# The second half of expert 1 for sequences 0 and 1, moved from the early stage into two more periods of the paired scheme

## The chip, the core and the metric

The kernel runs on one core of a Trainium2 chip. The metric is the time on the device in microseconds (us); of the kernel before, three runs are given, and one further execution was profiled. PE is the matrix engine (TensorE), DVE the VectorE, ACT the ScalarE, POOL the GpSimd; SP issues DMA transfers.

## What is computed

A gated linear attention, and then a mixture of experts with a balanced routing matrix. All numbers are float32 at the interface; the kernel splits each into two float16 parts ("high" and "low") and forms three products of four.

```python
# attention: batch 4, 8 heads, 768 tokens, head size 48
f = 1/(1 + exp(-f_logit))
state = f[:, :, t, :, None]*state + einsum('bhd,bhe->bhde', k[:, :, t], v[:, :, t])
y[:, :, t] = einsum('bhd,bhde->bhe', q[:, :, t], state)
# x: the 3072 tokens by 384 columns of all heads
P = exp(x @ w_gate - max)                  # 8 experts
for _ in range(8):                         # rows and columns brought to their sums in turn
    P /= P.sum(1, keepdims=True) + 1e-9;  P /= P.sum(0, keepdims=True) + 1e-9;  P *= N/E
for e in range(8):
    out += P[:, e:e+1] * (maximum(x @ w1[e], 0) @ w2[e])   # w1: 384x1024, w2: 1024x384
```

## The kernel before

**Three stages.** The attention stage goes through 24 items (a sequence has six, of 128 tokens each; a unit `u` is half a sequence, three items). It is paced by steps `g` of 0 to 208: every step advances each live item by one `yield`, and then calls `fill(n)`, which issues `n` units of plain expert work on PE, so that PE has work while the other engines carry out the attention. Items 3 to 23 start eight steps apart; item `i` runs its first ACT operation (`ft`) at step 23 + 8(i-3) and its score products (`aps`) twelve steps later. The second stage is the balancing of the routing matrix (`balance`, 38 steps: six, then four for each of eight iterations). Each iteration ends in a matmul `sk_c` that adds over the partitions what DVE has reduced into `sk_cs`; DVE takes up `sk_c` before the next iteration. Each of these steps also calls `fill` with 6.9 units, and goes on after the 38 for as long as there are units. The third stage is one loop of periods, listed in `ORDER`.

**The plain way and the paired way.** The plain way is matmul upon matmul: `moe` treats a unit of 384 tokens, with 9 matmuls of 384 columns for each of the hidden blocks `f` and 3 for each block and tile on the way back; `moe_tile` treats 128 tokens, and is used for units 0 to 2 (`TILED = 3`), because their tokens come late: a group of four hidden blocks is 36 matmuls of 128 columns, and the way back 3 matmuls of 384 columns for each block. A unit of `fill` is one matmul of 384 columns or three of 128. For each group, ACT writes the high part (`hh`) and DVE the low part (`hl`). The paired way does one half (`m`) of an expert for one sequence (`b`) in one period with fewer products: 15 slots of 6 matmuls of 256 columns (`kb_A` to `kb_F`), and three blocks of 42 matmuls of 192 columns (`kyps`, `kxps`), 216 matmuls in all; sums and differences of weights and tokens (`k1s`, `xs`) are made beforehand on POOL, and split into `k1h`, `k1l`, `xah`, `xal`.

**What goes which way.** Experts 0 and 1 go the plain way (they fill the attention stage), experts 2 to 7 the paired way: 6 x 2 x 4 = 48 periods. Of expert 1 the second half of the hidden blocks (`m = 1`) of sequences 2 and 3 also goes the paired way (`HALVED`), in periods 49 and 50. `plain(e, u)` tells `moe` how many of the eight hidden blocks are left for it.

**What sets the order.** The code's own order: `pin` and `mm` chain the instructions of an engine in the order in which they are written, so an engine that waits holds up all that is written behind it. `FILL` gives the units of each step from a step on, and the plain work may not run ahead of its tokens ("an expert is ahead of its tokens"). `load` brings one quarter of a weight matrix, has ACT make the high part and DVE the low (`w1l`, `w2l`, line 385); `SECONDAT` gives the steps of these two for the eight quarters of expert 1. In the balancing stage, when the first 14 pairs of `RAW` are done, the pool `kw` opens, and in the next step `prepare_w1` begins on two quarters of expert 2: sums on POOL, a maximum (`wmx`) and four low parts (`k1l`) on DVE.

Of the kernel before, what the change touches and what calls it, by code (L numbers as in the profile page):

```python
# [26 lines left out]
FT = FF // 128  # L27
# [51 lines left out]
END = 27  # L79
W1AT = (0, 1, 2, 3, 5, 9, 10, 11, 12, 21, 23, 25, 26)  # L80
W1AT0 = (16, 18, 19, 19, 22, 23, 23, 27, 27, 33, 35, 40, 41)
W2AT = (4, 22, 25, 25, 27, 29, 30, 35, 38)
W2AT0 = (0, 1, 1, 3, 3, 5, 5, 5, 7)
W2AT1 = (3, 8, 10, 12, 13, 13, 14, 14, 19)
# [7 lines left out]
CONVAT = (3, 6, 7, 9, 11)  # L92
LAST_EVENTS = {18: (('gs', 'C', 1, 1), ('gs', 'C', 1, 2), ('hl', 'C', 1)), 19: (('gs', 'C', 1, 3), ('gf', 'F', 2), ('gh', 1, 0), ('gh', 1, 1))}
ENDING = '.0.1.01.1..12.1.22..23.23.34343444'
HALVED = (2, 3)
ORDER = [(e, m, b) for e in range(2, NE) for m in range(2) for b in range(B)] + [(1, 1, b) for b in HALVED]
PAIRED = (0, 1, 2)
BY_POOL = (1,)
# [9 lines left out]
TS = CT * C  # L108
ONES = CT * NP * D * 4
LEADS = 23  # L110
FILL = ((0, 11.7), (1, 10.3), (2, 0), (3, 0), (5, 2), (6, 0), (7, 6), (8, 6), (9, 0), (10, 6), (12, 5.3), (15, 5.3), (17, 5.3), (23, 8.7), (30, 8.7), (43, 8.0), (195, 7))
LEAD = 6.9
FIRSTAT = ((0,), (0,), (0, 4), (0, 7), (1, 9), (5, 10))
SECONDAT = ((16, 17), (18, 20), (17, 18), (17, 21), (20, 21), (20, 22), (24, 24), (24, 25))
# [169 lines left out]
def fast(ctx, tc, qkf, vbd, wg, w1, w2, out, flag):  # L284
# [10 lines left out]
    def behind(ins, first):  # L295
        tc.add_manual_dep(
            ins.ins, first.ins.name,
            mybir.DependencyInfo(mybir.DependencyClass.NoSync, mybir.DependencyReason.DATA),
            reason="issue order")
# [3 lines left out]
    def pin(ins):  # L303
        engine = ins.ins.engine
        if fixed[0]:
            if engine in last:
                behind(ins, last[engine])
            last[engine] = ins
        return ins

    def mm(transpose=False, **kw):
        ins = (nc.tensor.transpose if transpose else nc.tensor.matmul)(**kw)  # L312
        if order:
            behind(ins, order[-1])
        order.append(ins)
# [6 lines left out]
    wctx, wctx0, wctx2, actx, pctx = (ExitStack() for _ in range(5))  # L322
    wp2 = wctx2.enter_context(tc.tile_pool(name="wp2", bufs=4, side="right"))
    wp1 = wctx.enter_context(tc.tile_pool(name="wp1", bufs=4, side="right"))
    wp0 = wctx0.enter_context(tc.tile_pool(name="wp0", bufs=8, side="right"))
    ap = actx.enter_context(tc.tile_pool(name="ap", bufs=2, side="right"))
    dp = ctx.enter_context(tc.tile_pool(name="dp", bufs=1, space=DRAM))
    psm = ctx.enter_context(tc.tile_pool(name="psm", bufs=2, space=PSUM))
# [7 lines left out]
    for h in range(2):  # L336
        nc.gpsimd.affine_select(
            out=mask[h * 64:(h + 1) * 64], in_=mask[h * 64:(h + 1) * 64],
# [27 lines left out]
    def xof(u):  # L366
        return [x[:, :, u % 2, :] for x in xt[u // 2]]

    def load(e, k, j):
        src = (w1 if k == 1 else w2)[e, j]  # L370
        n = 4 * (k - 1) + j
        if n < 6:
            raw = xp.tile([128, 1152], F32, name=f"w{k}r_{e}_{j}", tag=f"x{'hl'[n % 2]}{3 - n // 2}", bufs=1)[:, 0:768]
        else:
            raw = rp.tile([128, 768], F32, name=f"w{k}r_{e}_{j}", tag="wraw", bufs=3)
        raw = raw.rearrange("p (a f) -> p a f", f=256 if k == 1 else DM)
        nc.sync.dma_start(out=raw, in_=src)
        yield
        wh, wl = ((wp0 if e else wp1 if k == 1 else wp2).tile(list(raw.shape), F16, name=f"w{k}{q}_{e}_{j}", tag=f"w{q}") for q in "hl")
        scale = W1S if k == 1 else W2S  # L380
        pin(nc.scalar.activation(out=wh, in_=raw, func=AF.Copy, scale=scale))
        pair = [wh, None]
        ws[e][k - 1][j] = pair
        yield
        pin(nc.vector.scalar_tensor_tensor(out=wl, in0=raw, scalar=scale, in1=wh, op0=ALU.mult, op1=ALU.subtract))  # L385
        pair[1] = wl
# [10 lines left out]
    def plain(e, u):  # L397
        return FT // 2 if e == 1 and u // 2 in HALVED else FT

# [42 lines left out]
    tiles, put_off, owed = [0], [False], []  # L442

    def moe_tile(e, u, t):
        w1s, w2s = ws[e]
        if (u, t) not in ready:
            raise RuntimeError("an expert is ahead of its tokens")
        xh, xl = xof(u)
        ts = slice(t * 128, t * 128 + 128)
        h = []  # L450
        for g in range(2):
            ps = bank([128, 4, 128], f"hps_{e}_{u}_{t}_{g}")
            n = 0
            for q, x in ((0, xh), (0, xl), (1, xh)):
                for f in range(4 * g, 4 * g + 4):
                    a = w1s[f // 2][q]
                    fs = slice((f % 2) * 128, (f % 2) * 128 + 128)
                    for k in range(KT):
                        mm(out=ps[:, f % 4, :], lhsT=a[:, k, fs], rhs=x[:, k, ts], start=(n == 0), stop=(q == 1 and k == KT - 1), skip_group_check=True)
                        n += 1  # L460
                        if n < 36:
                            yield 1 / 3
            i = tiles[0] % FT
            tiles[0] += 1
            th, tl = (hp.tile([128, 2, 256], F16, name=f"h{q}_{e}_{u}_{t}_{g}", tag=f"k{q}{i // 6}{i % 6 // 3}{i % 3}").rearrange("p c t -> p (c t)") for q in "hl")
            pf = ps.rearrange("p f t -> p (f t)")
            pin(nc.scalar.activation(out=th, in_=pf, func=AF.Relu))

            def low(tl=tl, pf=pf, th=th):
                pin(nc.vector.scalar_tensor_tensor(out=tl, in0=pf, scalar=0.0, in1=th, op0=ALU.max, op1=ALU.subtract))  # L470

            if put_off[0]:
                owed.append(low)
            else:
                low()
            h.append([v.rearrange("p (f t) -> p f t", t=128) for v in (th, tl)])
            yield 1 / 3
        ps = bank([128, DM], f"yps_{e}_{u}_{t}")
        n = 0
        for f in range(FT):  # L480
            if len(owed) > 1 - f // 4:
                raise RuntimeError("a low part is owed")
            wh, wl = w2s[f // 2]
            hh, hl = (v[:, f % 4, :] for v in h[f // 4])
            for a, b in ((hh, wh), (hh, wl), (hl, wh)):
                mm(out=ps, lhsT=a, rhs=b[:, f % 2, :], start=(n == 0), stop=(n == 3 * FT - 1))
                n += 1
                if n < 3 * FT:
                    yield 1
        yr = rp.tile([128, DM], F32, name=f"yr_{e}_{u}_{t}", tag="yraw", bufs=3)  # L490
        pin(nc.scalar.activation(out=yr, in_=ps, func=AF.Copy))
        nc.sync.dma_start(out=yscr[e][u, t * 128:(t + 1) * 128], in_=yr)
        yield 1
# [596 lines left out]
        return (lambda: xq), lambda: sums(b), [x32[:, k].rearrange("p u t -> p (u t)") for k in range(KT)]  # L1090

    first = [load(0, 1 + n // 4, n % 4) for n in range(8)]
    second = [load(1, 1 + n // 4, n % 4) for n in range(8)]
    wgen = gate_weights()
    it = early_item(0)
    go(it)
# [22 lines left out]
    live, g = [it, nxt], 0  # L1119
    for n in range(2, 8):  # L1120
        at_steps(first[n], *FIRSTAT[n - 2])
    for n in range(8):
        at_steps(second[n], 4 + n, *SECONDAT[n])
    begin = {LEADS + STEPS * (i - 3): i for i in range(3, NT)}
    begin_tail = max(begin) + 17
    while live or g < max(begin):
# [14 lines left out]
        put_off[0] = g < PUTOFF  # L1141
        fill([n for at_, n in FILL if g >= at_][-1])
        go_all(g)
# [325 lines left out]
    for n, (e, m, b) in enumerate(ORDER):  # L1469
        part = n % 4  # L1470
        if n - part + 4 < PERIODS and part in (0, 2):
            e2, m2, _ = ORDER[n - part + 4]
            gen = prepare_w1(e2, 2 * m2 + part // 2)
            at_all(n, W1AT if n else W1AT0, gen)
        if n == 0:
# [214 lines left out]
```

## Time and profile before

| | |
|---|---|
| median of 3 runs | 1459.27 us (1458.95 to 1459.32) |
| the profiled execution: its own time | 1458.97 us |
| its span, first to last instruction | 1457.2 us |
| busy: PE, DVE, ACT, POOL | 1435.4, 1241.6, 1112.2, 1092.3 us |
| granted TensorE clock, mean | 0.997 |

The own time is 1.8 us more than the span, and 0.3 us below the median of the runs. An engine's busy time counts stretches in which at least one of its instructions runs; matmuls overlap each other, so that the time of one in a row is longer than the distance from one to the next.

### The profile page before, as it was taken

Reading aid. Unit: us, or ns where it says so; the run is one execution under the profiler, and the core shown is the slowest. Engines: PE = TensorE matmul, PEld = TensorE weight load, DVE = VectorE, ACT = ScalarE, POOL = GpSimd, SP = SyncE. Lnnn points to the kernel's source line nnn. Section 1 sums busy time; section 2 is a strip of 40 time slices with the busy share of each in tenths; the row PEclk is TensorE's granted clock in tenths of the full one; section 3 lists DMA queues with packets and bytes.
Section 4 is the critical chain, followed back from the end, with each engine's and each line's share of the span. In section 5 each row is a group of like instructions: output and inputs, shape, how many; then the busy total and the mean of one; then the engine's idle time right before and its main releaser. Section 6 shows DMA issues by size and latency. Waiting matters only on the chain.

```text
span 1457.2 us, 40795 instructions
## 1 busy us (share of the span) xinstructions
PE 1435.4 (99%) x16188; PEld 1267.0 (87%) x16188; DVE 1241.6 (85%) x2540; ACT 1112.2 (76%) x2492; POOL 1092.3 (75%) x1288
## 2 busy tenths in 40 slices
PE   7999999999999999999999999999999999999997
PEld 5788886666568899999999999999999999999997
DVE  8868878877868998888899898888888889888886
ACT  7767778875547778888888888888777787778874
POOL 3244665675625769999999999999888888888874
PEclk9999999999999999999999999999999999999999
DMA  9245544541111011222211111111000000000201
GB/s 265 84 113 132 120 110 126 124 120 47 65 49 35 24 40 47 56 62 61 61 55 58 49 50 45 41 51 49 23 23 24 23 23 23 13 15 20 77 13 69
DMA packets 82955, 90.54 MB, mean 62 GB/s; under 512 B 50017, under 2 KB 69601, under 8 KB 82754
## 3 DMA queue, kind: packets, MB, share of 16 engines
q1 hardware_dynamic: 82322, 87.25, 21.6%
q8 instruction: 128, 2.10, 0.6%
q14 instruction: 73, 0.60, 0.1%
q10 hardware_dynamic: 432, 0.59, 0.1%
HBM read 64.03 MB, written 14.16 MB: 54 GB/s over the span
## 4 chain that ended last, share of the span: by engine, by line
PE 73%; DVE 3%; ACT 1%; POOL 0%; issue 0%; ACTq 0%; POOLq 0%; DVEq 0%
PE kyps L312 29%; PE kb_A L312 9%; PE kb_B L312 8%; PE kb_D L312 6%; PE kxps L312 5%; PE kb_C L312 4%; PE yps L312 4%; PE hps L312 3%; PE kb_E L312 2%; PE kb_F L312 2%; DVE k1l L1228 0%; DVE kf L1538 0%; DVE kl L1569 0%; POOL k1s L1216 0%; DVE acc L1387 0%
## 5 line engine op out<-in xcount | busy, mean ns | idle before, releaser
L312 PEld LDWEIGHTS <-k1h 128*128 128x128 f16 x3000 | 282.5, 98 | 21.4 <-issue 1.1
L312 PE MATMUL kyps<-k2h,kgl 128*128 128x192 f16 x1188 | 292.3, 246 | 0.6 <-POOL kgl L1564 0.6
L312 PE MATMUL kyps<-k2h,kgh 128*128 128x192 f16 x1188 | 292.3, 246 | 0.1
L312 PE MATMUL kyps<-k2l,kgh 128*128 128x192 f16 x1188 | 292.2, 246 | 0.0
L312 PEld LDWEIGHTS <-kgh 128*128 128x128 f16 x2400 | 220.9, 98 | 7.2 <-issue 0.5
L1564 POOL TENSOR_TENSOR kgl<-kf,kgh 128x512 f16<-128x512 f32 x148 | 198.4, 1341 | 2.1 <-ACT kgh L1561 2.1
L1387 DVE SCALAR_TENSOR_TENSOR yy<-kyps,pes,part 128x192 f32<-128x192 f32 x270 | 111.5, 413 | 92.5 <-PE kyps L312 82.3
L1564 POOL TENSOR_TENSOR kgl<-kr,kgh 128x512 f16<-128x512 f32 x148 | 175.4, 1185 | 9.1 <-PE kyps L312 7.7
L1430 POOL TENSOR_TENSOR acc<-acc,yy 128x384 f32<-128x384 f32 x135 | 134.9, 1000 | 58.4 <-DVE yy L1387 58.4
L312 PEld LDWEIGHTS <-k1l 128*128 128x128 f16 x1500 | 146.8, 98 | 16.9
L312 PEld LDWEIGHTS <-kh 128*128 128x128 f16 x1200 | 112.6, 98 | 7.9 <-issue 1.3
L312 PEld LDWEIGHTS <-kgl 128*128 128x128 f16 x1200 | 117.4, 98 | 0.9 <-POOL kgl L1564 0.8
L312 PEld LDWEIGHTS <-w1h 128*128 128x128 f16 x1248 | 87.9, 98 | 27.1 <-issue 2.1
L312 PE MATMUL yps<-w2h,hl 128*128 128x384 f16 x336 | 110.1, 328 | 1.0 <-DVE hl L470 0.9
L312 PE MATMUL yps<-w2l,hh 128*128 128x384 f16 x336 | 110.0, 328 | 0.6 <-DVE w2l L385 0.6
L312 PE MATMUL yps<-w2h,hh 128*128 128x384 f16 x336 | 110.1, 328 | 0.2 <-ACT hh L420 0.2
L1515 ACT ACTIVATE cp<-kb_A 128x512 f32<-128x512 f32 x150 | 89.8, 599 | 17.5 <-DVE kb_A L1517 15.9
L1541 POOL TENSOR_TENSOR kr<-kr 128x256 f32<-128x256 f32 x100 | 75.6, 756 | 33.5 <-DVE xbl L1029 26.4
L312 PEld LDWEIGHTS <-hh 128*128 128x128 f16 x672 | 65.1, 99 | 37.2 <-issue 1.0
L1384 ACT ACTIVATE kyps<-kyps 128x192 f32<-128x192 f32 x148 | 47.7, 322 | 65.2 <-PE kyps L312 65.1
L1561 ACT ACTIVATE kgh<-kf 128x512 f16<-128x512 f32 x150 | 94.9, 633 | 1.7 <-DVE kf L1538 1.6
L1561 ACT ACTIVATE kgh<-kr 128x512 f16<-128x512 f32 x150 | 94.3, 629 | 0.6 <-DVE kr L1538 0.6
(323 smaller groups left out, 5383.6 us busy)
## 6 DMA issues: line engine op xcount, KB each, us to landing
q<-in_qkf_dram SPq DMA_DIRECT2D x23, 672.0 KB, 5.0
k1r<-in_w_dram SPq DMA_DIRECT2D x26, 384.0 KB, 3.0
k2r<-in_w_dram SPq DMA_DIRECT2D x26, 384.0 KB, 3.0
ys<-yr SPq DMA_DIRECT2D x48, 192.0 KB, 2.4
yb<-ys SPq DMA_DIRECT2D x48, 192.0 KB, 2.4
vr<-in_vbd_dram SPq DMA_DIRECT2D x24, 192.0 KB, 2.5
out_dram<-acc SPq DMA_DIRECT2D x21, 192.0 KB, 1.9
w1r<-in_w_dram SPq DMA_DIRECT2D x8, 384.0 KB, 9.4
```

What stands on the lines that cost most here:

```text
L312: ins = (nc.tensor.transpose if transpose else nc.tensor.matmul)(**kw)
L1384: pin(nc.scalar.activation(out=out, in_=in_, func=AF.Copy, **kw))
L1387: pin(nc.vector.scalar_tensor_tensor(out=y, in0=ps, scalar=p, in1=z, op0=ALU.mult, op1=ALU.add))
L1430: pin(nc.gpsimd.tensor_tensor(out=y, in0=y, in1=z.rearrange("p s d -> p (s d)"), op=ALU.add))
L1515: pin(nc.scalar.activation(out=fresh(ev[2]), in_=bk, func=AF.Copy))
L1541: pin((nc.gpsimd if ev[2] == 'P' else nc.vector).tensor_tensor(out=r[:, 0], in0=r[:, 1], in1=r[:, 0], op=ALU.subtract))
L1561: pin(nc.scalar.activation(out=hs['g', t][0][i], in_=hs['f' if i else 'r', t], func=AF.Copy))
L1564: pin((nc.vector if tag == str(PERIODS - 1) and ev[1] else nc.gpsimd).tensor_tensor(out=hs['g', t][1][i], in0=hs['f' if i else 'r', t], in ...
```

## The change

`HALVED` names all four sequences, so that `ORDER` has 52 entries. Of expert 1 the plain way then keeps only hidden blocks 0 to 3 everywhere; `moe_tile` learns of it by `plain`. The last two quarters of both weight matrices of expert 1 are no longer loaded and split ahead of the attention (`second` has four entries in place of eight), and the pool `wp0` is half as large. `FILL` hands out fewer units per step, and the slots `W1AT0` of the first period's weight work are spread anew.

```diff
-W1AT0 = (16, 18, 19, 19, 22, 23, 23, 27, 27, 33, 35, 40, 41)
+W1AT0 = (16, 18, 19, 19, 22, 23, 23, 25, 26, 26, 29, 37, 40)
-HALVED = (2, 3)
+HALVED = (0, 1, 2, 3)
 ORDER = [(e, m, b) for e in range(2, NE) for m in range(2) for b in range(B)] + [(1, 1, b) for b in HALVED]
-FILL = (..., (12, 5.3), (15, 5.3), (17, 5.3), (23, 8.7), (30, 8.7), (43, 8.0), (195, 7))
+FILL = (..., (12, 5.3), (15, 5.3), (17, 5.3), (23, 5.2), (43, 6.7), (107, 7.5), (195, 6.5))
-    wp0 = wctx0.enter_context(tc.tile_pool(name="wp0", bufs=8, side="right"))
+    wp0 = wctx0.enter_context(tc.tile_pool(name="wp0", bufs=4, side="right"))
     # moe_tile
-        for g in range(2):
+        fts = plain(e, u)
+        for g in range(fts // 4):
...
-        for f in range(FT):
-            if len(owed) > 1 - f // 4:
+        for f in range(fts):
+            if len(owed) > fts // 4 - 1 - f // 4:
...
-                mm(out=ps, lhsT=a, rhs=b[:, f % 2, :], start=(n == 0), stop=(n == 3 * FT - 1))
+                mm(out=ps, lhsT=a, rhs=b[:, f % 2, :], start=(n == 0), stop=(n == 3 * fts - 1))
     # weights of expert 1
-    second = [load(1, 1 + n // 4, n % 4) for n in range(8)]
+    second = {n: load(1, 1 + n // 4, n % 4) for n in (0, 1, 4, 5)}
...
-    for n in range(8):
+    for n in second:
         at_steps(second[n], 4 + n, *SECONDAT[n])
```

**DVE at steps 23 to 43, before.** What stands between item 3's scan `r` (and its reciprocal) and item 4's scan, the last row; `hl` belongs to the plain work, `w2l` to expert 1's weights.

```order
L470 SCALAR_TENSOR_TENSOR hl_0_2_1_1156<-hps_0_2_1_1108,hh_0_2_1_1155 128x512
L385 SCALAR_TENSOR_TENSOR w2l_2_1165<-w2r_2_711,w2h_2_1164 128x768
L747 SCALAR_TENSOR_TENSOR q_3_1021<-q_3_1021,r_1131 112x512
L748 SCALAR_TENSOR_TENSOR vlc_1136<-vr_1023,vhc_1135 128x384
L751 SCALAR_TENSOR_TENSOR q_3_1021<-ft_131,pi_132 112x512
L753 TENSOR_TENSOR q_3_1021<-q_3_1021 112x512
L385 SCALAR_TENSOR_TENSOR w2l_3_1169<-w2r_3_727,w2h_3_1168 128x768
L470 SCALAR_TENSOR_TENSOR hl_0_0_0_1252<-hps_0_0_0_1212,hh_0_0_0_1251 128x512
L470 SCALAR_TENSOR_TENSOR hl_0_0_1_1294<-hps_0_0_1_1255,hh_0_0_1_1293 128x512
L732 SCALAR_TENSOR_TENSOR r_1324<-ft_125,ind 112x512
```

The same place of the change:

```order
L748 SCALAR_TENSOR_TENSOR q_3_1006<-q_3_1006,r_1105 112x512
L749 SCALAR_TENSOR_TENSOR vlc_1110<-vr_1008,vhc_1109 128x384
L752 SCALAR_TENSOR_TENSOR q_3_1006<-ft_131,pi_132 112x512
L754 TENSOR_TENSOR q_3_1006<-q_3_1006 112x512
L471 SCALAR_TENSOR_TENSOR hl_0_2_1_1145<-hps_0_2_1_1092,hh_0_2_1_1144 128x512
L733 SCALAR_TENSOR_TENSOR r_1229<-ft_125,ind 112x512
```

Both `w2l` are gone, and one `hl` is left of three.

**DVE in the balancing stage, before.** From the third take-up of `sk_c` (its reciprocal) to the fourth, of eight; `xal` and `xmx` belong to the sums of the tokens.

```order
L1192 RECIPROCAL sk_cs<-sk_c_7545 128x8
L1193 SCALAR_TENSOR_TENSOR pe<-pe,sk_cs 128x24x8
L1029 TENSOR_TENSOR xal_7504<-xs_2_7314,xah_7503 128x768
L1184 TENSOR_REDUCE pe<-pe 128x24
L1185 RECIPROCAL sk_rs<-pe 128x24
L1187 TENSOR_TENSOR pe<-pe,sk_rs 128x24x8
L1188 TENSOR_REDUCE sk_cs<-pe 128x8
L1029 TENSOR_TENSOR xal_7504<-xs_2_7314,xah_7503 128x768
L1011 TENSOR_REDUCE xmx<-x_3_7347 128x1
L421 SCALAR_TENSOR_TENSOR hl_6_0_7603<-hps_6_0_7588,hh_6_0_7602 128x384
L421 SCALAR_TENSOR_TENSOR hl_6_1_7623<-hps_6_1_7606,hh_6_1_7622 128x384
L1192 RECIPROCAL sk_cs<-sk_c_7610 128x8
```

The same stretch of the change, without the two rows at its head, which are alike:

```order
L1229 SCALAR_TENSOR_TENSOR k1l_0_7058<-k1s_0_6985,k1h_0_7057 128x640
L1030 TENSOR_TENSOR xal_7061<-xs_2_6842,xah_7060 128x768
L1185 TENSOR_REDUCE pe<-pe 128x24
L1186 RECIPROCAL sk_rs<-pe 128x24
L1229 SCALAR_TENSOR_TENSOR k1l_0_7058<-k1r_0_6965,k1h_0_7057 128x256
L1188 TENSOR_TENSOR pe<-pe,sk_rs 128x24x8
L1189 TENSOR_REDUCE sk_cs<-pe 128x8
L1229 SCALAR_TENSOR_TENSOR k1l_0_7058<-k1r_0_6965,k1h_0_7057 128x384
L1030 TENSOR_TENSOR xal_7061<-xs_2_6842,xah_7060 128x768
L1012 TENSOR_REDUCE xmx<-x_3_6875 128x1
L1193 RECIPROCAL sk_cs<-sk_c_7159 128x8
```

The two `hl` are gone from here, and three of the first quarter's four low parts have come in; before, they stand three iterations later. All eight `k1l` of the two quarters now lie ahead of the last `sk_c`, where four did.

## Rows read from the trace of the kernel before

**Rows 1.** The page: busy time by engine, the chain that ended last.
```profile
PE 1435.4 (99%) x16188; PEld 1267.0 (87%) x16188; DVE 1241.6 (85%) x2540; ACT 1112.2 (76%) x2492; POOL 1092.3 (75%) x1288
PE 73%; DVE 3%; ACT 1%; POOL 0%; issue 0%; ACTq 0%; POOLq 0%; DVEq 0%
```

**Rows 2.** Timeline, first `ft` of item 3; first `aps` of items 4, 12 and 23.
```profile
56.40 0.62 ACT L725 ACTIVATE ft<-q 112x504 f32<-112x504 f32 x1
...
90.06 0.22 PE L312 MATMUL aps<-qh,kb 112*128 112x64 f16 x2
...
197.80 0.22 PE L312 MATMUL aps<-qh,kb 112*128 112x64 f16 x2
...
344.23 0.22 PE L312 MATMUL aps<-qh,kb 112*128 112x64 f16 x2
```

**Rows 3.** Windows: start:end, length; busy time (count) by engine; PE clock; DMA share; GB/s.
```profile
44.70:56.40 11.70, 11.70 (x195) 9.79 (x193) 8.96 (x17) 10.34 (x20) 2.67 (x4) 1.00 0.27 77
56.40:90.10 33.70, 32.81 (x468) 26.37 (x466) 27.74 (x43) 24.04 (x49) 15.29 (x14) 1.00 0.43 111
90.10:197.80 107.70, 107.37 (x1845) 90.77 (x1844) 84.51 (x160) 79.05 (x171) 59.71 (x65) 1.00 0.50 122
197.80:344.20 146.40, 145.82 (x1852) 101.13 (x1850) 118.01 (x230) 114.26 (x247) 90.28 (x99) 1.00 0.44 110
...
378.00:406.70 28.70, 28.17 (x179) 17.22 (x178) 27.12 (x63) 13.16 (x27) 21.13 (x34) 1.00 0.09 32
406.70:422.00 15.30, 15.30 (x97) 9.33 (x96) 6.56 (x13) 6.13 (x13) 2.33 (x5) 1.00 0.19 65
520.00:1120.00 600.00, 599.94 (x6410) 569.59 (x6408) 535.14 (x1124) 492.44 (x1130) 541.71 (x636) 1.00 0.17 48
```

**Rows 4.** PE's waits from 44 to 500 us: in all, times, longest.
```profile
PE ktp L312 <- DVE kb L624: 1.4, 1, 1.4
PE yps L312 <- DVE hl L470: 0.9, 2, 0.7
PE kyps L312 <- POOL kgl L1564: 0.6, 1, 0.6
PE kb_A L312 <- ACT cp L1515: 0.5, 1, 0.5
PE sk_c L312 <- DVE sk_cs L1188: 0.5, 1, 0.5
```

**Rows 5.** Timeline of PE, plain work in the tiled form.
```profile
105.79 0.83 PE L312 MATMUL hps<-xh,w1h 128*128 128x128 f16 x12
106.46 0.83 PE L312 MATMUL hps<-xl,w1h 128*128 128x128 f16 x12
```

**Rows 6.** The chain in order of time: a run of 72 matmuls of 384 columns.
```profile
411.48 11.70 PE hps L312 x72
```

**Rows 7.** Groups on DVE, 0 to 500 us: count, busy us, mean ns, idle before.
```profile
L829 DVE SCALAR_TENSOR_TENSOR sl<-st,sh 48x384 f16<-48x384 f32 (+1 forms) x42 | 34.8, 828 | 5.8 <-ACT sh L821 5.3
L470 DVE SCALAR_TENSOR_TENSOR hl<-hps,hh 128x512 f16<-128x512 f32 x36 | 24.6, 683 | 24.9 <-ACT hh L467 24.7
L385 DVE SCALAR_TENSOR_TENSOR w1l<-w1r,w1h 128x768 f16<-128x768 f32 x8 | 7.5, 949 | 0.1
L1228 DVE SCALAR_TENSOR_TENSOR k1l<-k1s,k1h 128x640 f16<-128x640 f32 x8 | 6.7, 841 | 0.0
L1228 DVE SCALAR_TENSOR_TENSOR k1l<-k1r,k1h 128x256 f16<-128x256 f32 (+1 forms) x8 | 4.9, 618 | 0.0
```

**Rows 8.** Timeline of DVE: the two `sl` of item 3.
```profile
80.51 2.56 DVE L829 SCALAR_TENSOR_TENSOR sl<-st,sh 48x384 f16<-48x384 f32 x2 [0.20 <-ACT sh L821]
```

**Rows 9.** Windows, as in rows 3, where the clock fell.
```profile
23.00:27.00 4.00, 1.99 (x21) 1.27 (x22) 3.90 (x5) 3.92 (x9) 1.41 (x1) 0.84 1.02 306
27.00:30.00 3.00, 3.00 (x38) 2.76 (x36) 2.97 (x6) 2.66 (x7) 1.56 (x3) 0.50 0.85 290
30.00:36.00 6.00, 6.00 (x82) 4.11 (x81) 5.38 (x10) 2.39 (x5) 1.99 (x3) 0.79 0.86 213
```

More of the change, by code (lines that the diff above doesn't have):

```diff
@@ L110 @@
 LEADS = 23
-FILL = ((0, 11.7), (1, 10.3), (2, 0), (3, 0), (5, 2), (6, 0), (7, 6), (8, 6), (9, 0), (10, 6), (12, 5.3), (15, 5.3), (17, 5.3), (23, 8.7), (30, 8.7), (43, 8.0), (195, 7))
+FILL = ((0, 11.7), (1, 10.3), (2, 0), (3, 0), (5, 2), (6, 0), (7, 6), (8, 6), (9, 0), (10, 6), (12, 5.3), (15, 5.3), (17, 5.3), (23, 5.2), (43, 6.7), (107, 7.5), (195, 6.5))
 LEAD = 6.9
@@ L485, in moe_tile @@
             for a, b in ((hh, wh), (hh, wl), (hl, wh)):
-                mm(out=ps, lhsT=a, rhs=b[:, f % 2, :], start=(n == 0), stop=(n == 3 * FT - 1))
+                mm(out=ps, lhsT=a, rhs=b[:, f % 2, :], start=(n == 0), stop=(n == 3 * fts - 1))
                 n += 1
-                if n < 3 * FT:
+                if n < 3 * fts:
                     yield 1
```

## Prediction, written before the changed kernel ran

> **What bounds the kernel now.** I read the page first: PE is busy for 1435.4 us, 99% of the span, and the chain that ended last runs through PE for 73% of the span [rows 1]. So the time is the sum of PE's matmuls, and a gain has to come from fewer or cheaper matmuls, as long as the engines behind PE follow. The windows say where they do. In the periods PE works 599.94 of 600 us while DVE, the next engine, is busy for 535.1, that is 89% [rows 3]; DVE at nine tenths is then no hindrance when the order suits it. In the attention stage PE is as full (107.37 of 107.70 us, 145.82 of 146.40), with DVE at 78 and 81%; least cover lies in the stretch from step 23 to 43 (PE 32.81 of 33.70, DVE 82%) and in the balancing (DVE 27.12 of 28.70, 94%, PE 28.17) [rows 3]. The borders of the stretches are those of steps 23, 43, 107 and 195: item 3's `ft`, and the `aps` of items 4, 12 and 23 [rows 2]. Where PE does wait, it waits on DVE most of all: 1.4 us for one `kb`, 0.9 for `hl`, 0.5 for `sk_cs` [rows 4]. What PE idles before that (such as at 23 to 27 us [rows 9]) lies ahead of anything that the change touches.
>
> **What it removes on PE.** Twelve matmuls of 128 columns start 0.67 us after the twelve before them (105.79 to 106.46) [rows 5], so one costs 0.056; 72 of 384 columns take 11.70 us [rows 6], so one costs 0.163. A tile of the tiled form loses one group: 36 x 0.056 + 12 x 0.163 = 2.01 + 1.95 = 3.96 us. Sequence 0 has six such tiles, sequence 1 three (unit 2): 9 x 3.96 = 35.6. Unit 3 goes by `moe` and loses 4 x 9 + 3 x 4 x 3 = 72 matmuls of 384 columns: 11.7. Together 47.3 us.
>
> The Trainium skill (TensorE: Matmul & The Clock Gate, section Back-to-back issue gap) gives about 81 ns a matmul at 128 columns for a sustained stream of weight load and matmul. By that figure, an estimate from the page alone, the 324 narrow matmuls would cost 8 us more and the saving would be 55 us; the trace shows 56 ns for just such pairs, and decides.
>
> **What it adds on PE.** 600 us hold 6410 matmuls [rows 3]; at 216 a period that is 20.22 us a period, and two are 40.4. The new periods are of the same make, their weights (expert 1, second half) are prepared for periods 49 and 50 as it is, so neither POOL nor DVE nor the queues get weight work on top; what each adds in additions and output transfers lies under its own 20 us. Net on PE: -47.3 + 40.4 = -6.9 us.
>
> **What the engines behind PE make of it.** The saving is cut from stretches, and in each DVE has to fit into less. A unit of `fill` is 0.165 us (3.96/24).
>
> Steps 23 to 43 lose 20 x 3.5 = 70 units, 11.5 us: PE goes from 32.8 to 21.3 us. This cut isn't free to be put elsewhere: with 24 units a tile for expert 1 instead of 48, unit 0 holds 216 units, and step 43 has handed out 217. DVE loses two `w2l` (0.95 each) and three `hl` (0.68) [rows 7]: 27.7 - 1.9 - 2.0 = 23.8. That is more than PE's 21.3: here DVE becomes the bound. Against it, DVE is also rid of two `w1l` (1.9 us) just ahead, where it was busy for 8.96 of 11.70 [rows 3], and can start by as much sooner. The stretch then takes between 23.8 - 1.9 = 21.9 and 23.8 us, against 21.3 + the 0.9 of idle there already: the extra wait is between 0 and 1.6. I take 1.0, since DVE can't be without any gap.
>
> Steps 43 to 107 lose 64 x 1.3 = 83 units (13.7 us; PE 93.7), steps 107 to 195 lose 44 (7.3; PE 138.5). DVE has 84.5 - 83 x 0.029 = 82.1 in the first (an `hl` of 0.68 for 24 units) and 117 in the second: 88 and 84%. The periods bear 89% at no wait; here the items' chains are longer, and 0.3 and 0.6 us were lost at 78 and 81%. Bounds 0 and 2 us; I take 0.5, near the periods' row.
>
> The balancing loses the other 84 units, 12 steps: it ends with the 38th step instead of the 50th. `kw` opens at step 8 instead of 20, so the second quarter's four `k1l` come before the last `sk_c`: 2 x 0.84 + 2 x 0.62 = 2.9 us [rows 7] on a DVE that is 94% busy there, with 1.6 us of its own free [rows 3]. What comes late next is `sk_cs`, and PE stands at `sk_c`, with all plain matmuls behind it. In the stretch after, 406.7 to 422, DVE was busy for 6.6 of 15.3 [rows 3]; that slack is what is cut away. Bounds: 0 (the early steps take it up) and 2.9; I take 1.0. The cut of 12 steps (13.8 us) is part of the 47.3 above. POOL's `k1s` also come earlier, among `xs`, but in this part POOL has 21.1 of 28.7 us of work and PE waits for neither until the periods: nothing, or as much as the two waits at the head of the periods once more (0.6 and 0.5) [rows 4].
>
> Loads: four transfers of 384 KB fewer, ahead of step 23, with PE not waiting for any: nothing.
>
> **Sum.** -47.3 + 40.4 + 1.0 + 0.5 + 1.0 = -4.4 us. The profiled execution took 1458.97, so 1454.6; that one was 0.3 below the median of the runs, so 1454.9 for a median.
>
> **Rivals.**
>
> *All of it is saved.* DVE's head start covers steps 23 to 43 and the balancing keeps its pace; then 1459.3 - 6.9 = 1452.4, and with the idle of that stretch gone too, 1451.5. For it speaks that DVE waits for `hh` through much of the attention (24.9 us ahead of `hl` alone [rows 7]); against it the two sums above, 23.8 over 21.3 and 94% plus 2.9.
>
> *DVE binds in all the compressed stretches.* The two `sl` of an item took 2.56 us at 80.5 [rows 8], on average they take 2 x 0.83 [rows 7]. If closer work made every pair take 2.56, DVE had 0.9 us more for each item, 7 us over the eight items of steps 43 to 107: 82.1 + 7.2 = 89.3 of 93.7, 95%, as in the balancing. With 1.6 in steps 23 to 43, 2 in the rest of the attention, 2.9 in the balancing: -6.9 + 6.5, so 1458.9. The Trainium skill (SBUF — State Buffer, section on who interferes with whom) has VectorE operations with two SBUF inputs and GpSimd operations shut each other out of a shared port for a whole instruction. The long `sl` agree with it, though no row tells what held them up.
>
> *Slower.* PE idles in steps 23 to 43 until its clock falls. It did so once: with 1.99 us busy of 4 the granted clock went to 0.50, the lower of its levels, 1.2 instead of 2.4 GHz [rows 9]. The three rows make 1.3 + 3.0 + 2.5 = 6.8 us at that level, which cost half of it, 3.4. It decides from where a gap as at 23 to 27 us stands in steps 23 to 43, some 2 us at one place (item 3's chain `am`, `st`, `sl` late by that much). Its price: the 2 us, the 3.4 for the clock, and the 2.9 of the balancing with 2 elsewhere: -6.9 + 10.3, so 1462.7. Against it: the 1.4 us wait for `kb` [rows 4] did not bring the clock down (1.00 in the stretch behind it [rows 3]), and DVE's excess is spread over 40 operations.
>
> *The change doesn't do what it says* is excluded by the count: 324 + 108 + 72 = 504 matmuls go, 432 come, and the program has 72 fewer.
>
> **Chances.** My forecast 0.50, all saved 0.20, DVE binds throughout 0.23, slower 0.07. About 0.2% (2.9 us) is what a measurement of this kernel can tell from no change. Below 1456.4 lie all of the second and most of the first, 0.71 together; within 2.9 us on either side the rest of the first and nearly all of the third, 0.23; slower 0.06. The range goes from 1451.2 (all saved, with the idle of steps 23 to 43) to 1458.4 (just short of the third rival's full price); for the likeliest case alone 1453 to 1456.5.
>
> **What the profile of the changed kernel would show.** The periods at 20.22 us, 52 of them, with PE without a gap: if not, the added term is wrong. The first `aps` of item 23, at 344.2 before [rows 2], at 312 to 314: 197 units of 0.165 us, less the waits; at 311.7 or sooner there are none. PE's waits for `hl`, `sl` or `am` at 56 to 80 us of 1 to 2.5 us together, and DVE over 95% busy there: right on steps 23 to 43; PE full there: the first rival. `sk_c` apart by more than 4.8 us and PE waiting for `sk_cs` for 1 us or more: right on the balancing. A clock below 1.00 after 36 us: the slower rival. I am wrong if PE gains waits that I priced at nothing: for POOL's `k1s` and ACT's `k1h` at the head of the periods, or for weights of expert 1.

## The result, and the profile after

| | before, run beside it | after |
|---|---|---|
| median of the runs | 1459.24 us | 1480.72 us (1478.99 to 1481.74, 4 runs) |
| ratio | | 1.0147, 95% interval 1.0132 to 1.0162 |
| span of the profiled execution | 1457.2 us | 1480.0 us (its own time 1481.74) |

The change is slower by 21.5 us; 4.3 us faster was forecast. The page of the kernel after, busy time by engine and the chain that ended last:

```profile
PE 1437.5 (97%) x16116; PEld 1273.3 (86%) x16116; DVE 1266.9 (86%) x2587; ACT 1130.8 (76%) x2541; POOL 1121.2 (76%) x1314
PE 83%; DVE 10%; ACT 4%; issue 2%; POOL 1%; DMA 0%; ACTq 0%; DVEq 0%; POOLq 0%; SPq 0%
```

PE carries out 72 matmuls fewer, as the change says, and yet is busy for 2.1 us longer than before; and it stands idle for 42.5 us (1480.0 - 1437.5) where it stood for 21.8 [rows 1]. DVE and ACT now hold 14% of the chain, where they held 4%. Windows of the kernel after, cut where the steps of [rows 3] lie now (23, 43, 107, 195; then part of the balancing, and the periods):

```profile
55.90:87.20 31.30, 24.35 (x331) 18.82 (x329) 23.57 (x39) 20.83 (x45) 14.21 (x15) 0.93 0.45 119
87.20:195.30 108.10, 98.66 (x1666) 81.10 (x1665) 85.45 (x156) 79.76 (x171) 61.06 (x65) 0.97 0.51 124
195.30:337.20 141.90, 140.19 (x1762) 96.02 (x1760) 119.44 (x230) 111.91 (x244) 90.13 (x98) 0.99 0.47 117
372.00:404.50 32.50, 27.56 (x172) 16.51 (x171) 29.99 (x63) 14.66 (x30) 27.30 (x38) 1.00 0.19 61
504.70:1104.70 600.00, 599.94 (x6410) 569.56 (x6408) 534.17 (x1123) 492.98 (x1130) 543.42 (x639) 1.00 0.17 48
```

The periods are as forecast, 6410 matmuls in 600 us at 20.22 us a period. All of the loss lies ahead of them, and most of it in steps 23 to 107, where PE is idle for 7.0 and 9.4 us and the clock is below 1.00. In the second of these rows DVE is busy for 79% of the time and ACT for 74%: neither is full, and PE waits all the same. What for, the waits of PE from 44 to 500 us tell (in all, times, longest):

```profile
PE yps L312 <- ACT hh L468: 8.9, 9, 1.9
PE yps L312 <- DVE hl L471: 7.4, 10, 3.0
PE sk_c L312 <- DVE sk_cs L1189: 4.9, 3, 3.0
PE yps L312 <- DVE hl L421: 1.7, 2, 0.9
```

Nine waits for `hh`, and nine halved tiles: one each. A timeline of the kernel after shows one of them, on PE, ACT and DVE (rows of the three engines put together; the number in brackets is the idle time before the row and what ended it):

```profile
154.76 0.83 PE L312 MATMUL hps<-xh,w1l 128*128 128x128 f16 x12
155.63 0.60 ACT L468 ACTIVATE hh<-hps 128x512 f16<-128x512 f32 x1
156.28 0.34 PE L312 MATMUL yps<-w2h,hh 128*128 128x384 f16 x1 [0.69 <-ACT hh L468]
156.46 0.33 PE L312 MATMUL yps<-w2l,hh 128*128 128x384 f16 x1
...
156.26 0.69 DVE L471 SCALAR_TENSOR_TENSOR hl<-hps,hh 128x512 f16<-128x512 f32 x1 [0.31 <-ACT hh L468]
157.01 0.34 PE L312 MATMUL yps<-w2h,hl 128*128 128x384 f16 x1 [0.23 <-DVE hl L471]
```

The last first-layer matmul of the tile ends at 155.59; ACT and DVE start as soon as they can; still PE stands for 0.69 us until `hh` is there, issues two matmuls, and stands for 0.23 us until `hl` is there. This is the chain of a tile by itself, with nothing late; at five of the nine tiles `hh` or `hl` came later than that. Between the starts 156.46 and 157.01 lie 0.55 us where a matmul of this kind takes 0.163: the wait costs 0.39, not 0.23, since the last matmul's end, which the record counts as busy, would have overlapped the next. So a tile with ACT and DVE free loses about 0.92 + 2 x 0.16 = 1.24 us. With two groups, as before, the second group's 36 matmuls (2 us) lay over the first group's `hh` and `hl`, and the first group's way back over the second's.

One of the two longest waits, 3.0 us at 61.6, is of another kind (the other, as long, is for `sk_cs` at 381.7). DVE's timeline of the kernel after:

```profile
58.70 1.21 DVE L733 TENSOR_TENSOR_SCAN r<-ft,ind 112x512 f32<-112x512 f32 x1
...
60.83 0.55 DVE L749 SCALAR_TENSOR_TENSOR vlc<-vr,vhc 128x384 f16<-128x384 f32 x1
61.30 1.22 DVE L752 TENSOR_TENSOR_SCAN q<-ft,pi 112x512 f32<-112x512 f32 x1
62.55 1.46 DVE L754 TENSOR_TENSOR q<-q 112x512 f32<-112x512 f32 x1
63.94 0.68 DVE L471 SCALAR_TENSOR_TENSOR hl<-hps,hh 128x512 f16<-128x512 f32 x1
```

This is the one `hl` that is left in the second piece of order shown for the change: before, it stood ahead of the products with `r`; with 5.2 units a step the plain work gets to that group later, and `hl` is written behind the rest of item 3's burst.

Behind some of the waits the clock fell. Windows of the kernel after, and the clock (the third number from the end):

```profile
66.00:69.40 3.40, 3.40 (x30) 3.06 (x29) 1.44 (x3) 2.45 (x6) 0.86 (x3) 0.50 0.92 220
86.50:89.86 3.36, 3.36 (x53) 2.84 (x52) 1.85 (x7) 1.14 (x3) 2.45 (x3) 0.50 0.01 3
175.22:178.60 3.38, 3.38 (x51) 2.88 (x50) 3.00 (x6) 0.00 (x0) 1.18 (x3) 0.50 0.53 165
195.70:199.08 3.38, 3.38 (x47) 2.47 (x44) 1.63 (x4) 0.24 (x1) 1.26 (x2) 0.50 0.28 65
```

Four stretches of 3.41 us at 0.50, the lower of its levels, 1.2 instead of 2.4 GHz, with PE busy throughout: half of 13.6 us, so 6.8 us. (A further one of 6.83 us, at 25 us, is in both kernels.) The account against the kernel before is then: 20.7 us more idle, 6.8 for the clock, -6.9 for the matmuls saved, and 2.2 us that are left, to make 22.8, the difference of the spans. They fit the matmuls in flight that count as busy: 16 more waits than before at 0.16 us each would be 2.6, an estimate.

### The profile page after: what moved, and what is told of

It is laid out like the page before. It is cut to its first block, busy times and chain, and to the rows that moved or that the text cites. A ratio compares the mean times of both kernels' runs of the same rounds, so it can differ in the third digit from the quotient of the medians.

```text
span 1480.0 us, 40789 instructions
## 1 busy us (share of the span) xinstructions
PE 1437.5 (97%) x16116; PEld 1273.3 (86%) x16116; DVE 1266.9 (86%) x2587; ACT 1130.8 (76%) x2541; POOL 1121.2 (76%) x1314
## 4 chain that ended last, share of the span: by engine, by line
PE 83%; DVE 10%; ACT 4%; issue 2%; POOL 1%; DMA 0%; ACTq 0%; DVEq 0%; POOLq 0%; SPq 0%
PE kyps L312 30%; PE kb_B L312 9%; PE kb_A L312 9%; PE yps L312 7%; PE kb_D L312 7%; PE kxps L312 5%; PE hps L312 5%; PE kb_C L312 5%; PE kb_E L312 2%; PE kb_F L312 2%; DVE sl L830 1%; PE aps L312 1%; DVE r L733 1%; DVE hl L471 1%; PE kvb L312 1%
## 5 line engine op out<-in xcount | busy, mean ns | idle before, releaser
L312 PEld LDWEIGHTS <-k1h 128*128 128x128 f16 x3120 | 293.7, 98 | 21.4 <-issue 0.9
L312 PE MATMUL kyps<-k2h,kgh 128*128 128x192 f16 x1236 | 304.0, 246 | 0.1
L312 PE MATMUL kyps<-k2h,kgl 128*128 128x192 f16 x1236 | 304.1, 246 | 0.0
L312 PE MATMUL kyps<-k2l,kgh 128*128 128x192 f16 x1236 | 304.1, 246 | 0.0
L312 PEld LDWEIGHTS <-kgh 128*128 128x128 f16 x2496 | 229.7, 98 | 7.5 <-issue 0.5
L312 PE MATMUL yps<-w2h,hl 128*128 128x384 f16 x288 | 95.5, 331 | 9.2 <-DVE hl L471 7.4
L312 PE MATMUL yps<-w2h,hh 128*128 128x384 f16 x288 | 95.2, 331 | 8.9 <-ACT hh L468 8.9
L312 PE MATMUL yps<-w2l,hh 128*128 128x384 f16 x288 | 95.3, 331 | 1.0 <-DVE w2l L385 1.0
L312 PEld LDWEIGHTS <-w1h 128*128 128x128 f16 x1008 | 74.1, 99 | 25.6 <-issue 2.4
L312 PEld LDWEIGHTS <-hh 128*128 128x128 f16 x576 | 55.6, 99 | 41.6 <-ACT hh L468 10.8
```

## The experiments

Two theories were tested. **A (cover)**: a halved tile has nothing that lies over its own `hh` and `hl`. **B (closer work)**: the smaller numbers of units bring the items' operations on DVE closer together, so that PE waits for them, whatever the tiles look like. The kernel before ran beside each at 1458.9 to 1459.0 us.

| run | what it is | us | ratio to before (95%) |
|---|---|---|---|
| e1_after_cover | after, with tiles covered | 1467.77 | 1.0062 (1.0045 to 1.0079) |
| e2_after_cover_bal | e1, other split with balancing | 1468.45 | 1.0068 (1.0052 to 1.0085) |
| e3_before_fill | before, with few units in steps 23 to 43 | 1473.05 | 1.0096 (1.0079 to 1.0113) |
| e4_before_uncovered | before, with tiles uncovered | 1491.85 | 1.0221 (1.0204 to 1.0238) |
| e5_cover_fill | e1, units of steps 23 to 43 placed anew | 1466.71 | 1.0053 (1.0037 to 1.0070) |
| e8_cover_fill_kvb | e5, `kvb` cleared earlier | 1462.15 | 1.0023 (1.0013 to 1.0033) |
| e7_cover_fill_kvb_prep | e8, weight work from step 13 | 1460.00 | 1.0009 (0.9999 to 1.0019) |
| e6_cover_nomax | e1, less work on DVE | 1463.70 | 1.0031 (1.0019 to 1.0042) |
| e9_cover_fill_kvb_prep_last | e7, `hl` products last | 1459.78 | 1.0006 (0.9997 to 1.0015) |
| e10_same_prep17 | e9, weight work from step 17 | 1458.29 | 0.9996 (0.9987 to 1.0005) |
| e11_after_last | after, `hl` products last | 1473.23 | 1.0096 (1.0081 to 1.0112) |
| e12_three | e10, three sequences halved | 1465.75 | 1.0045 (1.0031 to 1.0059) |

**e1: the cover given back.** `moe_tile` is cut in two, its first layer (`hidden`) and its second (`back`), and expert 1's first layer is issued ahead of another tile's second layer; nothing else changes. The part for units 1 and 2:

```diff
-            for t in range(TT):
-                for e in range(2):
-                    yield from moe_tile(e, u, t)
+            for t in range(TT):
+                yield from hidden(0, u, t)
+                yield from hidden(1, u, t)
+                yield from back(0, u, t)
+                yield from back(1, u, t)
```

> The change, with its one-group tiles taken apart: the first layer of expert 1's tile is issued ahead of other second-layer work (for unit 0, the second layer of the tile before; for units 1 and 2, the second layer of expert 0's tile), so that ACT's high part and DVE's low part have some 2 us of matmuls over them. The same instructions, the same fill units a step. Theory A (a tile with one group of hidden blocks has no matmuls of its own to lie over its high and low parts, so PE stands for both, tile after tile, and its clock falls): the waits of PE for hh and hl of the tiled form, 16.3 us together, fall to under 3 us, the three extra falls of the clock (5.1 us of time) go, and the time is 1454 to 1460 us. Theory B (DVE and ACT are too full in the shorter steps, whatever the order): PE waits as long at other places, and the time stays at 1474 or more.

It took 1467.77 us, 13 less than the change and 8.8 more than before: between the two. Its waits of PE:

```profile
PE kvb L312 <- DVE kvb L796: 3.9, 1, 3.9
PE sk_c L312 <- DVE sk_cs L1207: 3.3, 2, 2.9
PE yps L312 <- DVE hl L470: 3.0, 1, 3.0
```

The nine waits for `hh` are gone, and of the ten for `hl` only the one behind item 3's burst is left. So A holds for some 13 us, a new wait already taken off. The waits that went were 13.3 us: nine times the bare chain (0.92, so 8.3) and 5.0 in which ACT or DVE were late at these tiles; the cover takes away both. Less came back of the clock than theory A had: the four falls are gone, but one of 6.83 us and one of 3.41 came at other waits. What is left is B's, in few large pieces. The new wait is for `kvb` at 81.4; in the change PE, held up by three tiles, got there too late to wait. DVE's timeline there:

```profile
78.79 1.46 DVE L736 TENSOR_TENSOR_SCAN r<-ft,ind 112x512 f32<-112x512 f32 x1
...
82.26 1.22 DVE L755 TENSOR_TENSOR_SCAN q<-ft,pib 112x512 f32<-112x512 f32 x1
83.39 1.43 DVE L854 SCALAR_TENSOR_TENSOR xl<-yps,xh 96x384 f16<-96x384 f32 x4
84.84 0.17 DVE L795 MEMSET kvb<- 112x128 int32 x1
85.08 0.07 DVE L796 MEMSET kvb<- 112x8 int32 x1
```

Two memsets, 0.2 us together, that wait for nothing but their turn, stand behind some 6 us of item 5's burst and low parts `xl`, and PE behind them; then the clock was at half for 6.8 us.

**e2: the balancing at its old length.** `FILL` of e1 gives 6.55 instead of 7.5 units from step 107 on, so that 50 balancing steps are left.

> The same, and FILL from step 107 on gives 6.55 units instead of 7.5, so that the 84 units taken from the balancing go back to it and it has 50 steps again. Theory A, with the second part that I put at 1.0 us (DVE too full when the k1l of the second quarter move ahead of the last sk_c): PE's wait for sk_cs, 4.9 us in the change, falls under 1 us, and the time is 2 to 5 us below that of the run with the cover alone. Rival: the wait moves into the attention stage, where DVE then has 91% of the shorter steps, and the time is the same within 1.5 us or longer.

The wait for `sk_cs` went from 3.3 to 1.1 us, but PE now waited for `sl` 4.4 us (6 times) and for `am` 1.1 in the attention: 1468.45, no gain, as the rival said. Units taken from one stage to cover another are missed there.

**e3 and e4: each theory by itself, in the kernel before.** e3 hands out fewer units in steps 23 to 43 and more from 107 on; e4 has expert 1's tiles do a group's first layer and its way back, then the other group's. The edit of e3:

```diff
-FILL = (..., (23, 8.7), (30, 8.7), (43, 8.0), (195, 7))
+FILL = (..., (23, 5.2), (43, 6.7), (107, 9.74), (195, 7))
```

> The kernel before with the change's fill units up to step 107 (5.2 and 6.7 a step instead of 8.7 and 8.0), made up for by 9.74 from step 107 to 195: the steps that the change shortens are shortened as much, on tiles of two groups, and PE's work is the same as before. Theory A: within 3 us of the kernel before, since tiles of two groups cover themselves. Theory B (DVE can't follow in the shorter steps): 8 us or more above it, with PE waiting for DVE between 56 and 180 us.

> The kernel before with nothing changed but the order inside expert 1's nine tiles: first group of hidden blocks, its second layer, second group, its second layer. Each group then stands alone, as in the change, at the fill units of before. Theory A: 18 bare groups at 0.69 us for hh, 0.23 for hl and some 0.17 us that a wait hides in the pipelined matmuls, about 1.1 us each, so 20 us more than before (15 to 28 with falls of the clock). Theory B: under 4 us more, as DVE and ACT have slack in the long steps.

Waits of PE in e3:

```profile
PE yps L312 <- DVE hl L470: 5.5, 4, 4.1
PE kvb L312 <- DVE kvb L792: 4.5, 1, 4.5
```

and in e4:

```profile
PE yps L312 <- ACT hh L467: 18.6, 18, 1.9
PE yps L312 <- DVE hl L470: 6.3, 18, 1.5
```

e3 was slower by 14 us: the same two waits as in e1, 8.6 us, and two more stretches of 6.8 us at half the clock. (e3 keeps the two `w2l` in steps 23 to 43, so DVE has 1.9 us more to do there than in the change.) e4 was slower by 33 us where 20 were expected: 24.9 us of waits at 18 uncovered groups (nine tiles of two), 3.4 for two falls of the clock, and some 6 us in flight (36 waits of 0.16). Each theory alone makes the kernel before slower by more than the 6.9 us of matmuls that the change saves; both are true. (e4 bares 18 groups, the change nine.)

**e5, e8, e7 and e6: which operation is late.** e5 gives e1's units in steps 23 to 43 in another order, so that `hl` stands ahead of the burst; e8 moves the two memsets of `kvb` (`hold_kv`) to just behind that of `pib`, some ten rows ahead on DVE (the four `xl` counted singly); e7 lets `prepare_w1` begin later in the balancing. e6 is e1 without the twelve maxima `xmx` (set to a constant, so the scaling that they guard is left out).

```diff
-FILL = (..., (23, 5.2), (43, 6.7), ...)
+FILL = (..., (23, 8.0), (25, 4.0), (31, 6.5), (35, 3.3), (39, 6.0), (43, 6.7), ...)
```

```diff
                 pin(nc.vector.memset(held_banks['pi'], 0.0))
+                hold_kv()
...
-        if i >= MERGED and 'kv' not in held_banks:
...
```

```diff
-        if kw is not None and not prepared:
+        if kw is not None and not prepared and step >= 13:
```

> The changed kernel with the cover of the first experiment (1467.8 us) and with the same units of plain work in steps 23 to 43 handed out otherwise: 8 a step at first, so that the low part hl of sequence 0's third tile stands on DVE ahead of item 3's scan burst again, then 4, 6.5, 3.3 and 6. If the place of that hl in DVE's order is what costs (order theory): the 3.0 us wait of PE at 61.6 us goes, the 3.9 us wait for kvb at 81 us stays, 1464 to 1466. If DVE's amount of work in these steps binds whatever the order (volume theory): the wait turns up at another operation and PE's waits between 45 and 92 us stay at 6 to 8 us in sum, 1467 to 1468.5.

> The kernel of the run before this one, with the two memsets of kvb moved ahead on DVE, from behind item 5's burst and the low parts xl to just behind the memset of pib (8 rows). Order theory: the 3.9 us wait for kvb goes or shrinks below 1.5 us and with it the fall of the clock behind it (6.8 us at half, worth 3.4): 5 to 7 us less than the run before it, 1457 to 1460. Volume theory: PE waits 3 us or more for the next thing that stands behind the burst (am, then the chain st, sl), the clock falls all the same, less than 2 us gained.

> As the run before this one, with the first weight work of the periods (prepare_w1, eight k1l and two maxima on DVE) begun only from step 13 of the balancing, 5 steps later, where before the change it lay later too. If these low parts ahead of sk_cs make the 2.9 us wait for sk_c at 367 us: it goes down to 1.5 or less, without a fall of the clock behind it, 2 to 4 us less than the run before; the head of the periods stays as it is (waits under 1.5 us). If the balancing is late for other work on DVE (maxima, xal): within 1 us of the run before, or later at the head of the periods by 1 to 3 us.

> The cover of the first experiment (1467.8 us), with the twelve maxima xmx of the tokens left out (set once to a constant), most of which DVE takes in the balancing stage: this leaves out part of the scaling that guards the low parts. If DVE's fullness is what makes PE wait at sk_c (3.3 us, and a clock at half for 3.4 us behind it): waits for sk_cs under 1 us and no fall there, 3 to 5 us less, 1463 to 1465. If it is the single place of the low parts k1l ahead of one sk_cs: the wait at 367 us stays above 2 us, and less than 1.5 us is gained.

Waits of PE in e5:

```profile
PE sk_c L312 <- DVE sk_cs L1207: 5.6, 4, 2.0
PE kvb L312 <- DVE kvb L796: 2.4, 1, 2.4
```

and in e7:

```profile
PE sk_c L312 <- DVE sk_cs L1209: 2.8, 3, 1.2
```

e5 gained only 1.1 us: the 3.0 us wait went, and `hl` (1.8), `hh` (0.9) and `hl` again (0.3) took its place, with 2.4 for `kvb` and the fall of the clock behind it, and 5.6 for `sk_cs` in place of 3.3. PE's waits between 45 and 92 us are 6.1 in sum, as the volume theory said; the time lies between the two ranges, 0.3 below its own. e8 gained 4.6 us more, a little under the 5 to 7 of the order theory: the wait for `kvb` and the fall of the clock are gone, and nothing of its size took their place (0.7 for `al`). So placing the units anew mostly moved PE's waits to other operations, while moving one small operation ahead took a wait away. e7 took another 2.1: the waits for `sk_cs` are half of what they were. e6 gained 4.1 on e1, its waits for `sk_cs` down from 3.3 to 2.1 and no fall of the clock behind (one as long came at 65 us instead). The time is in the range for DVE's fullness, the wait between the two expectations, so DVE's fullness and the place of `k1l` may both count there.

**e9, e10 and e11: the products with `hl` last.** In the second layer the eight products with `hh` of four hidden blocks come ahead of their four with `hl` (`hl_last`), so that 1.3 us lie over `hl`; e11 does this alone, on the changed kernel. e10 is e9 with the weight work from step 17.

```diff
-            for a, b in ((hh, wh), (hh, wl), (hl, wh)):
...
+        for a, b, f in hl_last(fts):
```

> The last kernel (cover, order of the units, kvb ahead, weight work from step 13: 1460.0 us) with one more edit: in the second layer the products with hl stand behind all products with hh of the same four hidden blocks (8 matmuls, 1.3 us, lie over hl), in tiles and in units. PE there still waits 3.8 us for hl (0.3 and 1.8 between 68 and 81 us, 0.8 and 0.9 at 218 and 264). If these waits are PE's loss one for one: 2 to 3 us less, 1457 to 1458, under the 1459.0 of the kernel before. If DVE's chain sets the pace there and the wait only goes to the next step (kvps, am, sl): within 1 us of 1460.

> As the run before this one, with the first weight work of the periods begun at step 17 of the balancing instead of 13. If the low parts k1l still stand ahead of sk_cs (PE waits 1.2 us twice at 361 and 367 us): one of the two waits goes, 0.5 to 1.5 us less than the run before, 1456 to 1457.5. If the weights are then late for the first period: PE waits 1 us or more at its head (kb_A, kb_B) and the time is the same or up to 2 us more.

> The changed kernel as it is (1480.7 us), with the products with hl behind those with hh as in the first run of this batch, and nothing else. If the halved tile's own chain is the cost (first layer, hh, hl, and PE needs both at once): hh's wait stays (8.9 us), hl's 9.1 us go down to 3 us or less, together with what matmuls in flight hide: 4 to 9 us less, 1472 to 1477. If PE waits in these tiles because DVE is late as a whole, the wait for hl goes to another operation of DVE (sl, am, kvb): less than 2 us gained, 1479 to 1481.

Waits of PE in e11:

```profile
PE yps L312 <- ACT hh L471: 9.6, 9, 1.9
PE sk_c L312 <- DVE sk_cs L1189: 3.1, 1, 3.1
PE kvb L312 <- DVE kvb L793: 2.5, 1, 2.5
PE yps L312 <- DVE hl L474: 2.1, 1, 2.1
```

With one edit of order, e11 is 7.5 us faster than the change: the waits for `hl` at the tiles are gone, those for `hh` stay, one a tile; of the clock, one fall of 6.83 us has come and the four of 3.41 have gone. e9 gained 0.2 where 2 to 3 were expected: the 1.8 us for `hl` at 79 us went, and 1.2 for `xl` came, as its second alternative said: there DVE's chain sets the pace. e10 gained 1.5: one wait of 0.6 us for `sk_cs` is left, and 0.5 for `k1l` came at the head of the periods. It is level with the kernel before. The page of e10, and its wait for `sk_cs`:

```profile
PE 1430.2 (98%) x16116; PEld 1270.0 (87%) x16116; DVE 1265.3 (87%) x2587; ACT 1129.0 (78%) x2541; POOL 1118.7 (77%) x1314
```

```profile
PE sk_c L312 <- DVE sk_cs L1209: 0.6, 1, 0.6
```

PE is busy for 5.2 us less than before, most of the 6.9, and idle for 4.8 us more (1456.8 - 1430.2, against 21.8). What it waits for is small and scattered: `sl` 1.4 us, `hl` 1.2, a transfer into `kt` 1.1, `xl` and `hh` 0.9 each. Whether an arrangement of the same work exists that keeps the 6.9 us is open.

**e12: half the step.** Sequence 0 keeps both halves of expert 1, so steps 23 to 43 keep their 8.7 units; 51 periods.

```diff
-HALVED = (0, 1, 2, 3)
+HALVED = (1, 2, 3)
-FILL = (..., (23, 8.0), (25, 4.0), (31, 6.5), (35, 3.3), (39, 6.0), (43, 6.7), (107, 7.5), (195, 6.5))
+FILL = (..., (23, 8.7), (30, 8.7), (43, 7.7), (107, 7.2), (195, 6.5))
```

> The kernel of 1458.3 us with three sequences halved instead of four: of expert 1 sequence 0 keeps both halves in the plain way (as before the change), sequence 1 loses its second half to one more period, 51 in all. The units of steps 23 to 43 are those of before (8.7 a step), then 7.7 and from step 107 on 7.2. On PE that is 3 x 3.96 + 11.7 - 20.2 = 3.4 us less than before instead of 6.9. If the cut of steps 23 to 43 is what eats the gain (DVE has no room there, whatever the order): PE's waits between 45 and 92 us fall from 3 us to 1 us or less, and the time is 1455.5 to 1457.5, under the 1459.0 of the kernel before. If each compressed stretch takes its share of the gain instead, less compression with half the gain ends at the same place: 1457.5 to 1459.5, no difference from the kernel of 1458.3.

It took 1465.75 us (1463.53 to 1466.61), more than either expected. Its first window and its waits:

```profile
44.70:92.00 47.30, 47.30 (x726) 39.17 (x727) 37.06 (x66) 35.47 (x70) 18.45 (x20) 1.00 0.36 99
```

```profile
PE yps L312 <- DVE hl L426: 4.4, 3, 1.9
PE sk_c L312 <- DVE sk_cs L1209: 2.7, 2, 2.0
PE yps L312 <- ACT hh L425: 2.2, 2, 1.7
```

Up to 92 us PE has no gap: with the old units the two waits of steps 23 to 43 don't arise, as expected. But the units have shifted against the items: the ends of the halved units of `moe`, which too have only four hidden blocks, now meet DVE's bursts of `xal` and `xbl`: PE waits for `hl` for 1.6 and 1.9 us at 346, with a fall of the clock at 350, and for 1.0 at 364, and for `hh` for 1.7 at 236. In the profiled execution, whose own time is 1463.59, PE is idle for 6.6 us more than before; with 1.7 for that fall and -3.4 for the matmuls this makes 4.9, and its span is 4.7 longer. One of the other four runs is near it, and three are at 1466, for which there is no trace. A cover for `moe` like that for the tiles was not tried, so that the question of this run, what steps 23 to 43 alone cost, is answered by PE's waits there and not by the time.

## Why the prediction was wrong

**The matmuls were right.** -47.3 + 40.4 was counted rightly as far as the runs show it: the periods take 20.22 us, and e10, with most waits gone, has PE busy for 5.2 us less.

**The step that failed** is "A tile of the tiled form loses one group: 36 x 0.056 + 12 x 0.163 = 2.01 + 1.95 = 3.96 us." A group of the other half was also what PE did while ACT and DVE made the first group's `hh` and `hl`. Costed with that, a tile loses 1.24 us of its 3.96 at the least, and 9 tiles 11 us. e1 measured 13, with what ACT and DVE were late there and its part of the clock; e4 shows the same wait in the kernel before, with nothing removed. The sum named what hides the edits that it costed at nothing, but not what the removed work itself hid. That is also why the sums of busy time in "What the engines behind PE make of it" could not show it: at 79 and 74% neither DVE nor ACT is full in steps 43 to 107, and PE loses 14 us there: 9.4 of idle time, all at the six tiles of this stretch, 3.0 for the clock and 1.9 in flight (12 waits).

**By stretches** (us; the third column is the stretch before, less the units taken from it, as the prediction has them):

| stretch | before | before, less units | after | over |
|---|---|---|---|---|
| steps 23 to 43 | 33.7 | 22.2 | 31.3 | 9.1 |
| steps 43 to 107 | 107.7 | 94.0 | 108.1 | 14.1 |
| steps 107 to 195 | 146.4 | 139.1 | 141.9 | 2.8 |
| from there to the first `kb_F` of the periods | 97.3 | 83.5 | 88.3 | 4.8 |

Together 30.8 us over, where the forecast put 2.5; some 2 us came back outside these stretches.

In the first stretch "the extra wait is between 0 and 1.6", from DVE's 23.8 us of work over PE's 21.3, was mis-sized. DVE's busy time in it did come out at 23.6, but that is 75% of the stretch and not the 95% that was to show DVE as the bound: the sum took for granted that DVE's work fits in whatever order it stands. The waits of three bare tiles (0.9, 0.9 and 2.1), the `hl` behind the burst (3.0), 2.1 us for the falls at 66 and 86.5 and 1.1 in flight (7 waits) make 10.1; before, 0.9 us of idle time lay there. The slower rival, given 0.07, named the place and the clock rightly, though not the operation; it priced one gap of 2 us, and there were nine tiles besides. The longer `sl` of the rival in which DVE binds throughout came in part: the 16 of steps 43 to 107 took 16.4 us against 13.7 before, where it put 7 us more.

In the balancing "Bounds: 0 (the early steps take it up) and 2.9; I take 1.0": the place was right, PE waits for `sk_cs`, but for 4.9 us against 0.5 before, and mostly not behind the four `k1l` that the bound counted, those of the second quarter. PE's waits in the kernel after, and on DVE the first and the last of these four:

```profile
384.77 0.39 PE L312 MATMUL sk_c<-sk_cs,onesf 128*128 128x8 f32 x2 [3.05 <-DVE sk_cs L1189]
391.07 0.39 PE L312 MATMUL sk_c<-sk_cs,onesf 128*128 128x8 f32 x2 [1.52 <-DVE sk_cs L1189]
401.09 0.39 PE L312 MATMUL sk_c<-sk_cs,onesf 128*128 128x8 f32 x2 [0.37 <-DVE sk_cs L1189]
```

```profile
394.60 1.26 DVE L1229 SCALAR_TENSOR_TENSOR k1l<-k1s,k1h 128x640 f16<-128x640 f32 x1
400.95 0.55 DVE L1229 SCALAR_TENSOR_TENSOR k1l<-k1r,k1h 128x384 f16<-128x384 f32 x1
```

Only 0.37 us of the 4.9 lie there. The 3.05 lie where the first quarter's low parts stand now, three iterations earlier than before, among `xal`. The prediction put nothing on that move. No run moves the two quarters apart; e7 and e10, which begin the work on both quarters later and leave all else, cut the wait from 5.6 to 2.8, and from e9's 2.8 to 0.6.

The first `aps` of item 23 came at 337.2, not at 312 to 314; the clock fell after 36 us, the sign of the slower rival. Right were the 72 matmuls fewer, the loads, and the head of the periods, where the second and third are together 1.1 us shorter than before.

## What to carry to other kernels

Ahead of removing work from an engine that is the bound, write down what that work lies over: a matmul group saved is worth its own time less the latency of the next result that it hid (here 1.24 of 3.96 us a tile), and the busy shares of the other engines don't show that. Where the engines work strictly in the order of the code, as here, give each one-group chain another tile's matmuls in between, and put first what another engine waits for: two memsets, 0.2 us together, moved ahead by some ten rows, were worth 4.6 us. A table of units per step fixes not only how much cover a stage has, but also behind which burst each small operation stands; when a unit's length changes, read the order of the engines anew.

## What the runs showed of the hardware

The clock fell to its lower level for 3.41 or 6.83 us, no other length save at the program's very end, in all runs, also where no single wait was long: ahead of the falls at 175 and 196 us in the kernel after the waits were 1.2 and 1.0, and 1.7 and 0.2 us. Other waits of the same size had no fall behind them (3.0 us at 381.7 in the kernel after; 1.9 and 0.3 at 137). So the price of a wait of 2 to 4 us was either its own length or up to 3.4 us more, and which it was could not be told from its length. The Trainium skill (TensorE: Matmul & The Clock Gate, section A second HAM failure mode: psum-queue depth-cycling) tells of a kernel whose PE idles shortly but often between groups of matmuls until its clock goes up and down; the falls at 175 and 196 us agree with that, as far as two cases can.
